# Beta's loads on ScalarE's queue, the feature maps as tasks of their own, and a smaller allowance when few scores are ready, in a four-layer attention kernel

## The chip, the cores and the metric

The kernel runs on one core of one Trainium2 chip. The metric is the device time of one execution in microseconds (us). The engines are named as in the profile: PE (TensorE, matmuls), DVE (VectorE), ACT (ScalarE), POOL (GpSimd) and SP (the queue that issues most DMAs). [...]

## The reference

The input x has 2048 tokens of 512 features. Four layers follow each other, A, B, A, B, each as x = x + f(layernorm(x)). Both kinds have 32 heads of 16 features.

```python
# layer A: four segments of 512 tokens, a memory M, z carried from one to the next
p = softmax(q @ k.T * 0.25 + causal_mask)          # inside the segment
a_dot = p @ v
phi = lambda t: where(t > 0, t + 1, exp(t))
a_mem = (phi(q) @ M) / (phi(q) @ z + 1e-6)
o = g * a_mem + (1 - g) * a_dot                    # g = sigmoid(beta), one number per head
M, z = M + phi(k).T @ v, z + phi(k).sum(tokens)
# layer B: plain attention over all 2048 tokens
o = softmax(q @ k.T * 0.25) @ v
```

Each layer ends with a product with its output weights. Gates g come from beta, 32 numbers.

## The kernel before, in words

The program is written out by a planner in Python: it appends instructions to five lists, one per engine, and derives the waits from the buffers that they read and write. What follows is the planner's order, which is also the order on each engine.

**Units.** The work is paced by units of three score banks. A bank is 128 keys by up to 512 queries of one head; PE computes it (line 325 in all cases, from masked queries `qm` and keys KA or KB), ACT takes the exponential of up to three banks at once (line 1023), and two or three units later PE multiplies with the values into bank 6. Score banks alternate between banks 0 to 2 and 3 to 5, so PE can be at most one unit ahead of ACT. Units of an A layer are causally masked: their banks are 512, 512 (two pieces) or 256 wide, and POOL cuts the diagonal (line 1038). Units of a B layer are unmasked and all 512 wide. Some banks of B layers ("dx") go to DVE instead, which computes the exponential with a polynomial (lines 732 and 756 to 766). When a group of a head's banks is done, DVE transposes the sum (line 1083), and POOL and DVE normalise it and write it to `oT` (lines 1087 to 1111).

**Background tasks.** All else is a task, a Python generator that yields `(needs, pe, dve)` ahead of each step: the needs that must be met, its PE bank use and its DVE cost in ns. `task_A` and `task_B` do LayerNorm, the transposes of the normalised x by DMA, and the projections of a segment. A projection is four matmuls into bank 7, the only bank for background work while units run, and a copy by DVE (line 341). `task_A` then also makes the feature maps phi(K) and phi(Q) (`phi`, line 510): ACT takes an exponential of half of them into `amem` (line 513), and two units later DVE combines it (lines 515 and 516). `task_mem` reads the memory and updates it (lines 577 to 631). `task_out` adds the memory's part and does the output projection into x (lines 664 to 693). A task list sorted by hand-written numbers (`make_tasks`, line 852) sets who is asked first; outputs come first of all, then earlier segments.

**Allowances.** After each unit `credit` (line 842) adds an allowance for PE and DVE; tasks run while it lasts. For unmasked units, tasks with a PE bank are asked first (`background(True)`, line 1202), the rest after. If fewer than 24 banks are ready the state is `low` (line 1195): no dx, and the allowance is 2600 ns of DVE a unit, instead of 1300 for A and 1420 for B units. Where a later instruction needs something that no task has done yet, `bg_must` (line 822) runs tasks on the spot; `run_deferred` (line 1101) uses it before it overwrites `oT`, if the output projection that reads it has not been written out.

**Start.** SP issues the first four tiles of x, the weights of A, then beta twice (once as `bet` for all partitions, in four pieces as `betT`, lines 368 to 374), then the rest of x and the other weights. `gates` (line 408) computes the two forms of the gates right after the first segment's transposes and ahead of the copies of its first projections: on ACT and on DVE these copies stand behind the gates. Before the first unit 66 matmuls on a unit matrix keep PE busy.

Of the kernel before, what the change touches and what calls it, by code (L numbers as in the profile page):

```python
# [7 lines left out]
P = 128  # L8
# [204 lines left out]
class Builder:  # L213
# [142 lines left out]

    def setup(self):
        sc = self.sc
        xv = self.inp["A_x"][0].rearrange("(t p) d -> p t d", p=P)
        for a, b in [(0, 1), (1, 2), (2, 3), (3, 4), (4, 8), (8, 12), (12, 16)]:  # L360
            sc.add_dma("sp", (lambda a, b: lambda e: e.dma_start(self.x[:, a:b, :], xv[:, a:b, :]))(a, b), self.batch(),
                       writes=self.b_x[a:b])
            if a == 3:
                for i, nm in ((1, "A_wk"), (0, "A_wq"), (2, "A_wv")):
                    src = self.inp[nm].rearrange("(c p) f -> p c f", p=P)
                    sc.add_dma("sp", (lambda i, src: lambda e: e.dma_start(self.wA[:, :, i * D:(i + 1) * D], src))(i, src),
                               self.batch(), writes=[self.b_wA[i]])
                beta = self.inp["A_beta"]
                sc.add_dma("sp", lambda e: e.dma_start(self.bet[:, :], beta.partition_broadcast(P)), self.batch(), writes=[self.b_bet])
                bb = self.batch()  # L370
                for r in range(4):
                    src = bass.AP(tensor=beta.tensor, offset=beta.offset + 2 * r, ap=[[0, 32], [8, 4], [1, 2]])
                    sc.add_dma("sp", (lambda r, src: lambda e: e.dma_start(self.betT[32 * r:32 * r + 32, :, :], src))(r, src),
                               bb, writes=[self.b_betT] if r == 3 else [])
        for w, b, nm in ((self.woA, self.b_woA, "A_wo"), (self.wB, self.b_wB[0], "B_wqkv"), (self.woB, self.b_woB, "B_wo")):
            src = self.inp[nm].rearrange("(c p) f -> p c f", p=P)
            sc.add_dma("sp", (lambda w, src: lambda e: e.dma_start(w[:, :, :], src))(w, src), self.batch(), writes=[b])

        def pool(fn, writes, reads=()):
            self.op("pool", fn, reads=reads, writes=writes)  # L380
        pool(lambda e: e.memset(self.ident[:, :], 1.0), [self.b_ident])
        pool(lambda e: e.affine_select(self.ident[:, :], self.ident[:, :], pattern=[[-1, P]], compare_op=ALU.is_equal,
                                       fill=0.0, base=0, channel_multiplier=1), [self.b_ident], [self.b_ident])
        wu = self.new_alloc()
        for _ in range(66):
            self.mm(self.ps[:, 0:P], self.ident[:, :], self.ident[:, :], True, True, [self.b_ident], self.banks[0], wu)
        hm = self.hmask
        pool(lambda e: e.memset(hm[:, :], 1.0), [self.b_hm])
        pool(lambda e: e.affine_select(hm[:, :], hm[:, :], pattern=[[-16, 8]], compare_op=ALU.is_ge,
                                       fill=0.0, base=0, channel_multiplier=1), [self.b_hm], [self.b_hm])  # L390
        pool(lambda e: e.affine_select(hm[:, :], hm[:, :], pattern=[[16, 8]], compare_op=ALU.is_ge,
                                       fill=0.0, base=15, channel_multiplier=-1), [self.b_hm], [self.b_hm])

        self.par = self.nc.alloc_sbuf_tensor("par", [P, 2], dt.float32)
        self.b_par = Buf("par")
        for e_ in range(2):
            hv = hm[:, :].rearrange("p (r two) -> p two r", two=2)[:, e_, :]
            self.op("dve", (lambda e_, hv: lambda e: e.tensor_reduce(self.par[:, e_:e_ + 1], hv, axis=mybir.AxisListType.X,
                                                                     op=ALU.add))(e_, hv),
                    reads=[self.b_hm], writes=[self.b_par])  # L400
        va = self.VA[:, :, :, :].rearrange("p s t (h f) -> p (s t) h f", f=17)
        pool(lambda e: e.memset(va[:, :, :, 16:17], 1.0), [b for l in self.b_VA for b in l])
        for bk in (6, 7):
            b = self.banks[bk]
            b.alloc = -1
            self.op("dve", (lambda b: lambda e: e.memset(self.ps[:, b.col0:b.col0 + 512], 0.0))(b), bank=b, alloc=-1)
# [103 lines left out]
    def phi(self, src, bsrc, dst, bdst):  # L510

        et = self.amem[:, :, :, :].rearrange("p a b c -> p a (b c)")
        self.op("act", lambda e: e.activation(et, src, ACT.Exp), reads=bsrc, writes=self.b_amem)  # L513
        yield [("at", self.step + 2)], 0, 1130
        self.op("dve", lambda e: e.tensor_scalar(dst, src, 0.0, 1.0, op0=ALU.max, op1=ALU.add), reads=bsrc, writes=bdst)
        self.op("dve", lambda e: e.tensor_tensor(dst, dst, et, ALU.min), reads=self.b_amem + bdst, writes=bdst)

    def v_evac(self, vt, bv):
        def f(bank, al, o):
# [5 lines left out]
    def task_A(self, L, s):  # L525
        sl = s % 2
# [8 lines left out]
        slot = self.take_xT()  # L535
# [6 lines left out]
        for c in range(NCH):  # L542
            yield from self.proj_fm(self.wA, self.b_wA[1], 512, slot, c, self.KA[:, sl, c, :], self.b_KA[sl][c])
            self.flags.add(("K", L, s, c))
            yield from self.proj_fm(self.wA, self.b_wA[0], 0, slot, c, self.QA[:, sl, c, :], self.b_QA[sl][c])
            self.flags.add(("Q", L, s, c))
            if c == 0:
                for ti in range(4):
                    yield from self.proj_tm(self.wA, self.b_wA[2], 1024, slot, ti,
                                            self.v_evac(self.VA[:, sl, ti, :], self.b_VA[sl][ti]))  # L550
                self.flags.add(("V", L, s))
        if s < 3:
            prev = (L, s - 1) if s else (L - 2, 3)
            read = [("dma", ("amemT",) + prev + (3,))] if prev[0] >= 0 and prev[1] else []
            yield ([("mem",) + prev] if prev[0] >= 0 else []), 0, 0
            old = [o for b in self.b_phk for o in b.reads.values()]
            for c in range(NCH):
                self.dma_tr(self.phk[:, :, c * 128:(c + 1) * 128], self.KA[:, sl, c, :], [self.b_KA[sl][c]], [self.b_phkc[c]],
                            ("phk", L, s), old)
            for j in range(2):  # L560
                yield [("dma", ("phk", L, s))] + read, 0, 0
                a, ba = self.phk[:, 2 * j:2 * j + 2, :], self.b_phk[2 * j:2 * j + 2]
                yield from self.phi(a, self.b_phkc + ba, a, ba)
            self.flags.add(("phk", L, s))
        self.give_xT(slot)
        if s > 0:
            for c in (0, 2):
                yield [("op", L, s - 1), ("mem", L, s - 1)] + ([("dma", ("amemT", L, s - 1, 3))] if s > 1 else []), 0, 0
                yield from self.phi(self.QA[:, sl, c:c + 2, :], self.b_QA[sl][c:c + 2], self.phq[:, c:c + 2, :], self.b_phq[c:c + 2])
            self.flags.add(("phq", L, s))  # L570
        self.flags.add(("proj", L, s))

    def task_mem(self, L, s):

# [207 lines left out]
    def met(self, need):  # L782
# [3 lines left out]
        def ok(n):  # L786
            if n == "xT":
                return len(self.xT_free) > 0
            if n == "xn":
                return done(("xn", self.rr.get("xn", 0) % 2))  # L790
            if n[0] == "dma":
# [60 lines left out]
    def make_tasks(self):  # L852
        order = []
        for base in (0, 2):
            A, B = base, base + 1
            for s in range(4):
                order.append((base * 100 + s * 10 + 1, self.task_A(A, s)))
                order.append((base * 100 + s * 10 + 2, self.task_mem(A, s)))
                order.append((base * 100 + s * 10 + (13 if base or s > 1 else 5), self.task_B(B, s)))
                order.append((-10, self.task_out(A, s)))  # L860
                order.append((-5, self.task_out(B, s)))
        order.sort(key=lambda z: z[0])
# [291 lines left out]
    def attention(self):  # L1154
        self.flags = {("x", 0, s) for s in range(NSEG)}
        self.xT_free = [0, 1]
        self.dma_at, self.forcing = {}, False
        self.sel, self.pvq, self.deferred, self.qm_free = [], [], [], [0, 1, 2, 3]
        self.qm_late = []

# [11 lines left out]
        n = 0  # L1172
        while True:
# [23 lines left out]
            isA = items[0][0].kind == "A"  # L1197
            split = not self.low and not isA
            self.unit(n, items, self.dx_pick(items))
            self.credit(5 if self.low else 2 if isA else 3, 2600 if self.low else 1300 if isA else 1420)  # L1200
            if split:
                self.background(True)
            self.cr_dve -= self.pv_step(n)
# [51 lines left out]
```

## Time and profile before

| | us |
|---|---|
| median of 3 runs (lowest, highest) | 2148.92 (2148.39, 2151.72) |
| the profiled execution, its own time | 2149.91 |
| its span, first to last instruction | 2148.0 |
| ACT busy in it | 2008.6 |
| PE busy | 1789.5 |
| DVE busy | 1593.3 |
| POOL busy | 407.0 |
| ACT waiting for PE's scores | 97.9 |
| mean granted PE clock | 0.694 |

A row of the profile's groups or timeline has the engine, the line of the kernel, the operation, what it writes and reads, and in brackets how long the engine sat idle before it and what ended that. The busy time of a merged row is the sum without overlaps. In the table by stages each stage has its length and then busy time and number of instructions for PE, PE's weight loads, DVE, ACT and POOL, then the granted PE clock, the share of the DMA engines' time, and GB/s. A wait row gives the sum, the number and the longest wait.

### The profile page before, as it was taken

To read this page: it belongs to the slowest core of one execution; us is meant where nothing else is said; L and a number is where in the kernel's file an instruction comes from. 1 tells how busy PE (TensorE), PEld (TensorE's weight loads), DVE (VectorE), ACT (ScalarE), POOL (GpSimd) and SP (SyncE) were. 2 spreads that over 40 slices of the span, in tenths; PEclk is the share of its full clock that TensorE was granted. 3 is DMA by queue.
4 is the path that set the end of the run, shared out by engine and by line. 5 is a ranking of instruction groups with operands and counts; after the bars stand their busy time and mean duration, and the time that the engine had idled before them with its cause. 6 is when DMAs were issued, how large, how long until landed. Compare 5 with 4: busy or idle time off the path is not lost.

```text
span 2148.0 us, 30875 instructions
## 1 busy us (share of the span) xinstructions
PE 1789.5 (83%) x11634; PEld 414.1 (19%) x11634; DVE 1593.3 (74%) x2806; ACT 2008.6 (94%) x1618; POOL 407.0 (19%) x832
## 2 busy tenths in 40 slices
PE   7788888888788787787877888888888888888888
PEld 3222222211211212212222112221111111111111
DVE  6655665487658885688857975548799989988996
ACT  5788998999989999899998998889999999999997
POOL 3532433020150002400033102501100000000000
PEclk9889888756957968769866558785655565556555
DMA  4011000000000000000000001000000000000000
GB/s 138 16 25 21 20 14 13 6 1 13 8 1 11 1 13 9 11 11 1 15 11 6 1 3 19 11 11 1 11 1 1 1 11 1 1 1 11 1 1 11
DMA packets 67125, 24.54 MB, mean 11 GB/s; under 512 B 59808, under 2 KB 66464, under 8 KB 66976
## 3 DMA queue, kind: packets, MB, share of 16 engines
q1 hardware_dynamic: 66976, 22.57, 4.6%
q8 instruction: 91, 1.49, 0.3%
q14 instruction: 58, 0.48, 0.1%
HBM read 6.30 MB, written 2.10 MB: 4 GB/s over the span
## 4 chain that ended last, share of the span: by engine, by line
issue 39%; ACT 28%; PE 19%; DVE 9%; POOL 4%; DMA 1%; SPq 0%; POOLq 0%; ACTq 0%; DVEq 0%
ACT pT L1023 27%; PE ps L325 19%; POOL ob L1096 1%; POOL pT L1038 1%; POOL qm L941 1%; DVE tT L1083 1%; DVE VB L341 1%; DVE VA L341 1%; DVE dxt L732 1%; DMA xT<-xn 1%; DVE QB L341 0%; ACT amem L513 0%; DVE x L686 0%; DVE lnst L431 0%; DVE QA L341 0%
## 5 line engine op out<-in xcount | busy, mean ns | idle before, releaser
L1023 ACT ACTIVATE pT<-ps 128x1536 bf16<-128x1536 f32 (+2 forms) x1589 | 1985.8, 1439 | 111.1 <-PE ps L325 97.9
L325 PE MATMUL ps<-qm,KB 32*128 32x512 bf16 x4096 | 682.5, 524 | 235.3 <-ACT pT L1023 217.6
L325 PE MATMUL ps<-pT,VB 128*17 128x512 bf16 x3716 | 664.8, 515 | 23.7 <-DVE tT L1083 18.3
L1096 POOL TENSOR_TENSOR ob<-tT,rd 128x256 bf16<-128x256 f32 x128 | 99.8, 780 | 1207.5 <-DVE rd L1087 1168.3
L732 DVE TENSOR_SCALAR dxt<-ps 128x512 uint32<-128x512 f32 x380 | 261.0, 687 | 86.3 <-PE ps L325 80.3
L325 PEld LDWEIGHTS ps<-qm,KB 32*128 32x128 bf16 x4096 | 133.8, 96 | 762.9 <-ACT pT L1023 679.6
L1038 POOL TENSOR_SCALAR_AFFINE_SELECT pT<-pT 128x256 bf16<-128x256 bf16 (+2 forms) x512 | 210.2, 427 | 322.4 <-ACT pT L1023 313.1
L766 DVE SCALAR_TENSOR_TENSOR dxo<-dxt,dxz 128x1024 int16<-128x1024 uint16 (+1 forms) x203 | 235.1, 1158 | 4.6
L325 PEld LDWEIGHTS ps<-pT,VB 128*17 128x17 bf16 x3716 | 119.1, 90 | 520.3 <-issue 452.9
L325 PE MATMUL ps<-dxo,VB 128*17 128x512 bf16 x380 | 205.4, 541 | 0.4 <-DVE dxo L766 0.4
L325 PE MATMUL ps<-qm,KA 32*128 32x512 bf16 (+3 forms) x1024 | 127.5, 376 | 39.6 <-ACT pT L1023 31.8
L760 DVE TENSOR_TENSOR dxz<-dxz,dxo 128x1024 f16<-128x1024 f16 (+1 forms) x203 | 135.1, 666 | 4.3
L325 PE MATMUL ps<-pT,VA 128*17 128x512 bf16 (+3 forms) x1024 | 121.2, 378 | 18.5 <-DVE tT L1083 10.9
L756 DVE TENSOR_SCALAR dxo<-dxt 128x1024 f16<-128x1024 uint16 (+1 forms) x203 | 132.9, 655 | 2.2 <-PE ps L325 2.0
L764 DVE TENSOR_TENSOR dxz<-dxz,dxo 128x1024 f16<-128x1024 f16 (+1 forms) x203 | 131.8, 649 | 2.1
L1083 DVE STREAM_TRANSPOSE tT<-ps 128x512 f32<-128x512 f32 x112 | 79.7, 712 | 70.6 <-PE ps L325 70.4
L941 POOL TENSOR_SCALAR qm<-QB,par 128x512 bf16<-128x512 bf16 x102 | 81.6, 808 | 180.2 <-PE ps L325 179.9
L758 DVE TENSOR_SCALAR dxz<-dxo 128x1024 f16<-128x1024 f16 (+1 forms) x203 | 88.7, 437 | 6.8
L325 PE MATMUL ps<-xT,wB 128*128 128x512 bf16 x256 | 82.9, 433 | 9.2 <-DMA xT<-xn 2.5
L686 DVE TENSOR_TENSOR x<-x,ps 128x512 bf16<-128x512 bf16 x64 | 44.0, 688 | 60.2 <-PE ps L325 60.0
L762 DVE TENSOR_SCALAR dxz<-dxz 128x1024 f16<-128x1024 f16 (+1 forms) x203 | 83.7, 412 | 6.7
L325 PE MATMUL ps<-xT,wA 128*128 128x512 bf16 x256 | 78.6, 419 | 10.3 <-DVE QA L341 5.3
(89 smaller groups left out, 917.9 us busy)
## 6 DMA issues: line engine op xcount, KB each, us to landing
out_dram<-x SPq DMA_DIRECT2D x8, 256.0 KB, 2.1
x<-in_A_x_dram SPq DMA_DIRECT2D x3, 512.0 KB, 10.9
wB<-in_B_wqkv_dram SPq DMA_DIRECT2D x1, 1536.0 KB, 12.7
xT<-xn SPq DMA_TRANSPOSE x60, 2.5
x<-in_A_x_dram SPq DMA_DIRECT2D x4, 128.0 KB, 2.4
wA<-in_A_wk_dram SPq DMA_DIRECT2D x1, 512.0 KB, 4.4
wA<-in_A_wq_dram SPq DMA_DIRECT2D x1, 512.0 KB, 5.5
wA<-in_A_wv_dram SPq DMA_DIRECT2D x1, 512.0 KB, 6.3
```

Of the source, the lines that this page charges most:

```text
L325: self.sc.add("pe", lambda e: e.matmul(out, lhsT, rhs, start=start, stop=stop, skip_group_check=True), reads=reads, banks=[(bank, "w", all ...
L732: self.op("dve", lambda e: e.tensor_scalar(self.dxt[:, b, i, :], o, SCALE * LOG2E * 65536, 127.0 * 65536, op0=ALU.mult, op1=ALU.add), writ ...
L756: self.op("dve", lambda e: e.tensor_scalar(f, lo, 2.0 ** -16, None, op0=ALU.mult), reads=bt, writes=bo)
L758: self.op("dve", lambda e: e.tensor_scalar(z, f, EXP_C3, EXP_C2, op0=ALU.mult, op1=ALU.add), reads=bo, writes=bz)
L760: self.op("dve", lambda e: e.tensor_tensor(z, z, f, ALU.mult), reads=bo + bz, writes=bz)
L764: self.op("dve", lambda e: e.tensor_tensor(z, z, f, ALU.mult), reads=bo + bz, writes=bz)
L766: self.op("dve", lambda e: e.scalar_tensor_tensor(ob, hi, 128.0, z, op0=ALU.mult, op1=ALU.add), reads=bt + bz, writes=bo)
L941: self.op(eng, (lambda m, q, col: lambda e: e.tensor_scalar(m, q, col, 0.0, op0=ALU.mult, op1=ALU.add))(m, q, col), reads=[bq, self.b_par] ...
L1023: self.sc.add("act", (lambda dst, src: lambda e: e.activation(dst, src, ACT.Exp, scale=SCALE))(dst, src), writes=self.b_pT[slot * 3 + i:sl ...
L1038: self.op("pool", (lambda blk, pat: lambda e: e.affine_select(blk, blk, pattern=pat, compare_op=ALU.is_ge, fill=0.0, base=0, channel_multi ...
L1083: self.op("dve", lambda e: e.transpose(tT.rearrange("p a b -> p (a b)"), src), reads=bsrc, writes=[bt], bank=bk, alloc=al)
L1096: self.op("pool", lambda e: e.tensor_tensor(ob, tT[:, :, 0:16], rb, ALU.mult), reads=[bt, br], writes=[self.b_ob[oi][g.e]])
```

## The change

1. The five loads of beta are issued by ACT as its first instructions, instead of by SP between the weights and the rest of x.
2. The feature maps leave `task_A` for a task of their own, `task_phi`, sorted right behind it. A half may begin only two units after the half before it was combined (`"phi"`). `task_A` gives its buffer of transposed x back before the feature maps rather than after those of K. Layer 1's tasks for segments 0 and 1 are now asked ahead of `task_phi` and `task_mem` of the same segment; before they were asked behind `task_mem`.
3. In the state `low` the allowance is 1900 ns of DVE a unit instead of 2600.

```diff
     def setup(self):
         sc = self.sc
+        beta = self.inp["A_beta"]
+        bb = self.batch()
+        for r in range(4):
+            src = bass.AP(tensor=beta.tensor, offset=beta.offset + 2 * r, ap=[[0, 32], [8, 4], [1, 2]])
+            sc.add_dma("act", (lambda r, src: lambda e: e.dma_start(self.betT[32 * r:32 * r + 32, :, :], src))(r, src),
+                       bb, writes=[self.b_betT] if r == 3 else [])
+        sc.add_dma("act", lambda e: e.dma_start(self.bet[:, :], beta.partition_broadcast(P)), self.batch(), writes=[self.b_bet])
...
-                sc.add_dma("sp", lambda e: e.dma_start(self.bet[:, :], beta.partition_broadcast(P)), self.batch(), writes=[self.b_bet])
-                bb = self.batch()
-                for r in range(4):
-                    src = bass.AP(tensor=beta.tensor, offset=beta.offset + 2 * r, ap=[[0, 32], [8, 4], [1, 2]])
-                    sc.add_dma("sp", (lambda r, src: lambda e: e.dma_start(self.betT[32 * r:32 * r + 32, :, :], src))(r, src),
-                               bb, writes=[self.b_betT] if r == 3 else [])
...
         self.op("dve", lambda e: e.tensor_tensor(dst, dst, et, ALU.min), reads=self.b_amem + bdst, writes=bdst)
+        self.phi_at = self.step
...
+        self.give_xT(slot)
+        self.flags.add(("KQ", L, s))
+
+    def task_phi(self, L, s):
+
+        sl = s % 2
+        yield [("KQ", L, s)], 0, 0
         if s < 3:
...
-                yield [("dma", ("phk", L, s))] + read, 0, 0
+                yield [("dma", ("phk", L, s)), "phi"] + read, 0, 0
...
-        self.give_xT(slot)
         if s > 0:
             for c in (0, 2):
-                yield [("op", L, s - 1), ("mem", L, s - 1)] + ([("dma", ("amemT", L, s - 1, 3))] if s > 1 else []), 0, 0
+                yield ["phi", ("op", L, s - 1), ("mem", L, s - 1)] + ([("dma", ("amemT", L, s - 1, 3))] if s > 1 else []), 0, 0
...
+            if n == "phi":
+                return self.bubble or self.forcing or self.step >= self.phi_at + 2
...
-                order.append((base * 100 + s * 10 + 2, self.task_mem(A, s)))
-                order.append((base * 100 + s * 10 + (13 if base or s > 1 else 5), self.task_B(B, s)))
+                order.append((base * 100 + s * 10 + 2, self.task_phi(A, s)))
+                order.append((base * 100 + s * 10 + 3, self.task_mem(A, s)))
+                order.append((base * 100 + s * 10 + (14 if base or s > 1 else 1.5), self.task_B(B, s)))
...
-            self.credit(5 if self.low else 2 if isA else 3, 2600 if self.low else 1300 if isA else 1420)
+            self.credit(5 if self.low else 2 if isA else 3, 1900 if self.low else 1300 if isA else 1420)
```

The arithmetic is the same. The changed program has the same operations but for the planner's choices: 376 instead of 380 banks go to DVE.

More of the change, by code (lines that the diff above doesn't have):

```diff
@@ L367, in setup @@
                                self.batch(), writes=[self.b_wA[i]])
-                beta = self.inp["A_beta"]
-                sc.add_dma("sp", lambda e: e.dma_start(self.bet[:, :], beta.partition_broadcast(P)), self.batch(), writes=[self.b_bet])
-                bb = self.batch()
-                for r in range(4):
-                    src = bass.AP(tensor=beta.tensor, offset=beta.offset + 2 * r, ap=[[0, 32], [8, 4], [1, 2]])
-                    sc.add_dma("sp", (lambda r, src: lambda e: e.dma_start(self.betT[32 * r:32 * r + 32, :, :], src))(r, src),
-                               bb, writes=[self.b_betT] if r == 3 else [])
         for w, b, nm in ((self.woA, self.b_woA, "A_wo"), (self.wB, self.b_wB[0], "B_wqkv"), (self.woB, self.b_woB, "B_wo")):
@@ L564, in task_A @@
             self.flags.add(("phk", L, s))
-        self.give_xT(slot)
         if s > 0:
             for c in (0, 2):
-                yield [("op", L, s - 1), ("mem", L, s - 1)] + ([("dma", ("amemT", L, s - 1, 3))] if s > 1 else []), 0, 0
+                yield ["phi", ("op", L, s - 1), ("mem", L, s - 1)] + ([("dma", ("amemT", L, s - 1, 3))] if s > 1 else []), 0, 0
                 yield from self.phi(self.QA[:, sl, c:c + 2, :], self.b_QA[sl][c:c + 2], self.phq[:, c:c + 2, :], self.b_phq[c:c + 2])
             self.flags.add(("phq", L, s))
-        self.flags.add(("proj", L, s))
     def task_mem(self, L, s):
@@ L1156, in attention @@
         self.xT_free = [0, 1]
-        self.dma_at, self.forcing = {}, False
+        self.dma_at, self.forcing, self.phi_at = {}, False, -9
         self.sel, self.pvq, self.deferred, self.qm_free = [], [], [], [0, 1, 2, 3]
```

## The prediction, made before the changed kernel ran

> **What bounds the kernel now.** I read the page first, then ScalarE's (ACT's) waits, then the busy time of each stage, then the timeline of the stages that lose time. The page says which engine sets the end:
>
> ```profile
> span 2148.0 us, 30875 instructions
> ...
> PE 1789.5 (83%) x11634; PEld 414.1 (19%) x11634; DVE 1593.3 (74%) x2806; ACT 2008.6 (94%) x1618; POOL 407.0 (19%) x832
> ```
>
> ACT works 2008.6 of 2148.0 us, nearly all of it exponentials of scores. So the time is ACT's work plus ACT's idle time, 139.4 us, and an edit counts only as far as it changes one of the two. ACT's waits name what ends the idle time:
>
> ```profile
> ACT pT L1023 <- PE ps L325: 97.9, 137, 4.2
> ...
> ACT omgT L414 <- DMA betT<-in_A_beta_dram: 5.0, 1, 5.0
> ...
> ACT amem L513 <- DVE phk L516: 3.3, 2, 3.0
> ```
>
> Mostly scores come late from TensorE (PE); the wait for beta and the wait of one half feature map for the other are the two that the change aims at. The table by stages shows where the idle time lies (a stage's length less its ACT column; PEclk is the granted clock):
>
> ```profile
> 17.80:32.06 14.26, 11.87 (x66) 3.24 (x65) 9.00 (x24) 7.92 (x7) 3.98 (x11) 0.78 0.64 217
> ...
> 90.72:129.03 38.31, 26.62 (x177) 6.66 (x177) 25.64 (x64) 23.16 (x26) 19.24 (x49) 0.79 0.14 28
> 129.03:344.60 215.57, 186.38 (x1334) 50.76 (x1334) 125.85 (x262) 192.79 (x181) 77.04 (x184) 0.82 0.11 21
> ...
> 578.73:624.01 45.28, 34.52 (x268) 9.31 (x270) 20.33 (x43) 39.74 (x43) 32.34 (x79) 0.52 0.00 1
> ...
> 1145.74:1406.78 261.04, 221.96 (x1415) 50.18 (x1410) 184.52 (x328) 242.89 (x199) 53.91 (x107) 0.70 0.04 7
> ```
>
> Idle: 14.7 us before the first score at 17.80, then 6.3, 8.8 (to 90.72), 15.2, 22.8, and 18.2 in the last row. The long stage 1441 to 2137 idles 3.7 of 695 us, so nothing can be won there. I follow the change by units (unit n is the n-th set of three score banks); the order of the changed program's instructions tells what PE and VectorE (DVE) do between two units.
>
> **Start, units 0 to 5.**
>
> ```profile
> 10.93 1.89 PE L325 MATMUL ps<-xT,wA 128*128 128x512 bf16 x8 [0.87 <-DVE gtok L416]
> ...
> 15.62 0.21 ACT L414 ACTIVATE omgT<-betT 128x8 f32<-128x8 bf16 x1 [5.02 <-DMA betT<-in_A_beta_dram]
> 15.73 0.58 ACT L339 ACTIVATE QA<-ps 128x512 bf16<-128x512 f32 x1
> ...
> 17.14 0.61 PE L325 MATMUL ps<-qm,KA 32*128 32x512 bf16 x3 [4.32 <-DVE qm L941]
> 17.69 1.89 PE L325 MATMUL ps<-wA,xT 128*128 128x512 bf16 x4
> 17.80 1.45 ACT L1023 ACTIVATE pT<-ps 128x1536 bf16<-128x1536 f32 x1 [1.49 <-PE ps L325]
> ```
>
> Behind the exponential that waits for betT stand QA's copy on ACT and, on DVE, KA's copy and the masked queries. The Q projection ends at 10.93+1.89 = 12.8. With beta there, QA's copy ends at 13.4, the first masked query 0.4 later, scores follow at 13.9 instead of 17.14, and the first exponential at 14.4: 3.4 us earlier. What is late next is PE itself. Its pause shrinks from 4.3 to 1.1 us. In this trace the clock is 0.50 from 17.1 to 23.9 and 1.00 after; at 0.50 the four V matmuls take 1.89 and the scores 0.61, later 1.04 and 0.39. Three units at the full clock save 3 x (0.85+0.22) = 3.2. Together -6.6; walking the new DVE order (three operations a unit for the next segment's statistics, not five to nine) through these durations puts unit 6 at 25.4 instead of 32.06, the same. The other end: ACT now issues five DMAs first, 0.5 us each by SP's rows, over long before its first work at 9.45; SP loses five issues, so x's later tiles start some 2.9 us earlier, which nothing waits for. But bet lands at 4.25+5.9 = 10.2 and the last betT at 15.6: four transfers of 0.5 KB take 5.4 us. If they hold up the first four x tiles (issued from 0.8 to 2.2, 2.4 us to landing) by half of it, 2.7, the term is -3.9; by all of it, 5.4, the first score comes at 19.8 at the low clock: +2.
>
> [...]
>
> **Feature maps, halves apart.** Row 3.3+0.4 us of ACT waits. 3.0 of it is unit 59: there the scores for unit 60 ended at about 121.0 while ACT was free at 119.7, so 1.3 stays: -1.8. (Bounds 0 and -3.7.)
>
> **Smaller allowance.** Around 92 to 102 us PE waits 4.25 for QA's copy behind the next layer's LayerNorm on DVE; ACT loses 4.2+2.8+1.5 = 8.5. The new order has 28 DVE operations in five units where 29 stood in four. By their durations QA's copy ends at 95.9, the next scores at 97.7, and 6.7 is still lost: -1.7 (bounds +2, -6).
>
> **What the own task moves.** A half map needs 1130 of the DVE allowance; in unmasked units tasks with a PE bank are served first and spend it. So in segments 1 and 2 of layer 0 the last half map waits until the next masked units: the memory steps move from units 75 and 147 to 97 and 161, and the output projection, which came one a unit, must now be forced before oT is overwritten: in the new order sixteen woA matmuls stand in a row, twice; nowhere before. What one costs:
>
> ```profile
> 164.34 1.04 PE L325 MATMUL ps<-woA,oT 128*128 128x512 bf16 x4
> ...
> 165.41 0.69 DVE L686 TENSOR_TENSOR x<-x,ps 128x512 bf16<-128x512 bf16 x1 [0.27 <-PE ps L325]
> ...
> 166.16 1.04 PE L325 MATMUL ps<-woA,oT 128*128 128x512 bf16 x4
> ```
>
> One bank, so four matmuls, DVE's addition, the next four: a period of 1.82. Four end after 3 x 1.82+1.04 = 6.5; with weighted sums and the next scores (0.95) less one exponential (1.35), ACT idles 6.1. Two projections within one unit near 1312 cost ACT 2.51,
>
> ```profile
> 1311.65 1.04 PE L325 MATMUL ps<-wA,xT 128*128 128x512 bf16 x4 [0.54 <-DVE VA L341]
> ...
> 1313.48 1.04 PE L325 MATMUL ps<-wA,xT 128*128 128x512 bf16 x4 [0.79 <-DVE VA L341]
> ...
> 1315.14 2.43 ACT L1023 ACTIVATE pT<-ps 128x512 bf16<-128x512 f32 x3 [2.51 <-PE ps L325]
> ```
>
> and the same sum gives 1.82+1.04+0.8-0.96 = 2.7 for them. Two bursts 12.2, less the 2.1 that the spread outputs cost now: +10.1. Memory steps 1 and 2 stand among masked units, whose exponentials are shorter (1.2 a unit): step 3, which stands so now, costs 2.8, those among unmasked units 0.2. I take 1.8 each, +3.2; step 3 moves the other way, -2. Layer 0's projections of segments 2 and 3 move to unmasked units: by the idle before the units concerned 6.6 to 3.6, -3; layer 1's, with more whole projections in one unit, +0.7 and -1. Stage sum +8 (bounds +2, +17).
>
> **Layer 2.** Its memory steps 1 and 2 begin 7 units later and lie partly among unmasked units: idle 2.0+6.2 to about 5.7, -2.5 (0, -4). In the stage from 1146 the doubled projections of 1312 no longer occur (-2.5), one start after a pause goes (-1.3), and memory step and projections interleave at half a projection a unit (4.8 to 3.1): -5.5 (0, -8).
>
> **ACT's own work.** Counting the order: 376 scores on DVE instead of 380, so 4 more banks on ACT, and other cuts of the masked units: +9 of 1024 columns, +10 of 256, +10 of 768, +2 of 1536, -40 of 512. With 1.04, 0.40, 0.83, 1.36 and 0.54 us a piece: +2.8; by columns alone +1.8. I take +2.
>
> **Sum.** -6.6-1.8-1.7+8-2.5-5.5+2 = -8.1. The profiled execution took 2149.9 (span 2148.0 and 1.9 around it), 1.0 above the median of 2148.92; so 2141.8 by its own time and 2140.8 by the median. I forecast 2141. About 0.2%, 4.3 us, can be told from no change.
>
> **Rivals.**
> 1. Held-up start: the first term is -0.4 to +2 instead of -6.6, 2147 to 2150. For it: 5.4 us for 2 KB. Against: only what comes before the fourth tile's landing near 4.6 matters, when not all four can be through.
> 2. Layer 2 gives nothing (the dx queries on POOL, 2.3 to 3.6 a stage there, remain): -0.1, 2149.
> 3. The low clock, on the slow side: the moved stretch loses PE's clock. After each burst some ten units carry no projection, and such stages show 0.52 (578 to 624) though PE is 76% busy. At the low clock a burst costs 4 x 2.67-0.8 = 9.9 before scores, 9.5 idle: +6.8; memory steps 3 each, +2.4; the seven whole projections a unit from unit 130 at 2.67 instead of 1.82, +5.9. -8.1+15.1 = +7.0, 2156. It decides once bursts and projections both run cold (+12.7; +12.4 is the point for slower).
> 4. The change does not do what it says: the order shows all three parts done; only the halves' distance grows to 17 units.
>
> [...]
>
> **Chances.** Forecast, 2133 to 2146: 0.58; held-up start 0.13; layer 2 0.14; low clock 0.12; else 0.03. Faster 0.60, within 0.2% 0.27, slower 0.13. The range 2133 to 2151 takes in the first three.
>
> **What would show it.** Right: first exponential near 14.4 and clock 1.00 from 14 to 24; two ACT waits of about 6 where sixteen woA matmuls stand; no wait of amem for phk; idle in the stage that ends with unit 205 near 31, from 1146 on near 13. Wrong: x's first four tiles landing after 6 us, bursts with 1.89 a projection, or ACT work off by over 3.

## The result and the profile after

The changed kernel takes 2171.7 us (median of six runs, 2166.9 to 2178.9) beside 2151.6 for the kernel before: a ratio of 1.0097, 95% interval 1.0077 to 1.0118. It is 1% slower. I had forecast 2141 and a range that ended at 2151.

The profiled execution took 2166.89, the least of the six; its span is 2165.2, 17.2 us more than before, while the medians lie 20.1 apart. The first rows of the profile's page say whether ScalarE (ACT) worked longer or waited longer:

```profile
span 2165.2 us, 30735 instructions
...
PE 1782.1 (82%) x11539; PEld 418.4 (19%) x11634; DVE 1581.5 (73%) x2790; ACT 2011.8 (93%) x1609; POOL 400.8 (19%) x828
```

ACT works 3.2 us more than before and idles 153.4 us instead of 139.4. So the loss is idle time, as the bound of the prediction wants it. The table by stages, cut at the same units as in the prediction (the columns are those of that table), shows where:

```profile
18.75:30.16 11.41, 9.01 (x65) 2.88 (x64) 9.00 (x24) 7.80 (x8) 4.47 (x11) 1.00 0.55 202
88.63:122.96 34.33, 25.00 (x176) 6.58 (x177) 23.31 (x54) 22.33 (x25) 18.65 (x48) 0.85 0.16 32
122.96:360.57 237.61, 191.98 (x1308) 52.77 (x1326) 125.37 (x269) 193.19 (x171) 77.31 (x183) 0.76 0.10 19
...
597.04:642.06 45.02, 34.84 (x268) 9.42 (x270) 20.68 (x43) 39.79 (x43) 32.44 (x79) 0.54 0.00 1
1164.09:1419.00 254.91, 214.96 (x1418) 51.88 (x1428) 177.83 (x321) 243.32 (x192) 51.40 (x109) 0.75 0.04 8
```

A row's length less its ACT column is ACT's idle time: 3.6 (6.3 before), 12.0 (15.2), **44.4 (22.8)**, 5.2 (5.5) and 11.6 (18.2). Every one of these rows but one got better. The long stage of units 64 to 205 got worse by 21.6, and that is the result. In elapsed time against the kernel before, cut at the same units:

| part of the program | forecast | measured |
|---|---|---|
| until the first exponential of scores | -3.4 | +1.0 |
| units 0 to 63 | -6.7 (-3.2, -1.8, -1.7) | -7.0 |
| units 64 to 295 | +8 | **+23.6** (+22.0 to unit 205, +1.5 after) |
| units 296 to 1047 (the rest of layer 1, layer 2) | -2.5 and -5.5 | -5.4 (+1.8 to unit 746, -7.2 after) |
| the last 450 units, and ACT's own work | +2 | +5.1 |
| sum | -8.1 | +17.2 |

**The start.** On ACT's queue beta does come first, and x pays for it: its first four tiles land 4.7 us (median) after their issue, 2.4 in the kernel before. Rows of the first 19 us of the changed kernel (its line 1032 is line 1023 of before, 950 is 941, 692 is 686), and behind them the row of the kernel before in which the statistics of the fourth tile of x start:

```profile
0.80 1.87 ACTq L363 DMA_DIRECT2D betT<-in_A_beta_dram  x4
...
7.23 0.69 DVE L431 BATCH_NORM_STATS2 lnst<-x 128x6 f32<-128x512 bf16 x1 [1.02 <-DMA x<-in_A_x_dram]
...
11.15 1.03 PE L329 MATMUL ps<-ident,xn 128*128 128x128 bf16 x8 [3.42 <-DVE xn L464]
...
11.98 1.06 PE L329 MATMUL ps<-ident,oT 128*128 128x128 bf16 x8
...
14.30 2.94 PE L325 MATMUL ps<-xT,wA 128*128 128x512 bf16 x7 [1.26 <-DVE omgT L416]
...
17.28 0.60 ACT L339 ACTIVATE QA<-ps 128x512 bf16<-128x512 f32 x1 [3.81 <-PE ps L325]
...
18.75 1.45 ACT L1032 ACTIVATE pT<-ps 128x1536 bf16<-128x1536 f32 x1 [0.88 <-PE ps L325]
```

```profile
5.73 0.66 DVE L431 BATCH_NORM_STATS2 lnst<-x 128x6 f32<-128x512 bf16 x1
```

VectorE (DVE) waits for the third tile of x until 7.23, where it had all four by 5.73 before. TensorE (PE) pauses for 3.4 us instead of 0.8 after its 66 matmuls, and its clock falls (0.50 from 10.0 to 16.8 us): the transposes take 1.03 and 1.06 instead of 0.72 and 0.72, and the seven projection matmuls that the trace has take 2.94, 0.42 each, where eight took 1.89.

**The two rows of sixteen woA matmuls (the bursts) and one more wait.** First the stretch of unit 109, then SP's queue ahead of unit 127, then the stretch of unit 173:

```profile
190.85 1.04 PE L325 MATMUL ps<-woA,oT 128*128 128x512 bf16 x4 [0.78 <-DVE x L692]
191.92 0.69 DVE L692 TENSOR_TENSOR x<-x,ps 128x512 bf16<-128x512 bf16 x1 [1.13 <-PE ps L325]
...
194.15 10.77 ACT L1032 ACTIVATE pT<-ps 128x1536 bf16<-128x1536 f32 x11 [5.97 <-PE ps L325]
...
214.98 2.50 SPq L348 DMA_TRANSPOSE xT<-xn  x2
217.58 5.14 SPq L348 DMA_TRANSPOSE phk<-KA  x4
...
224.15 1.06 ACT L513 ACTIVATE amem<-phk 128x1024 bf16<-128x1024 bf16 x1 [4.37 <-issue]
...
299.28 1.89 PE L325 MATMUL ps<-woA,oT 128*128 128x512 bf16 x4 [0.78 <-DVE x L692]
...
301.95 1.89 PE L325 MATMUL ps<-woA,oT 128*128 128x512 bf16 x4 [0.78 <-DVE x L692]
...
307.17 9.62 ACT L1032 ACTIVATE pT<-ps 128x1536 bf16<-128x1536 f32 x10 [9.47 <-PE ps L325]
```

Four matmuls, DVE's addition, the next four: a period of 1.82 in the first burst, 2.67 in the second, where the clock is at 0.50. ACT waits 5.97 and 9.47. Between them stands a wait that I had not seen coming: ACT's exponential of phi(K) waits 4.37, though the profile names no engine for it ("issue"). The rows above it tell what it is: the four transposes into phk occupy SP's queue from 217.58 to 222.7, and they stand there behind two transposes of another task, from 214.98 to 217.48. KA, which they read, had long been there: the order has its last projection in unit 101 and the request in unit 124.

### The profile page after: what moved, and what is told of

Read it like the earlier page. It is cut to its first block, busy times and chain, and to the rows that moved or that the text cites. A ratio compares the mean times of both kernels' runs of the same rounds, so it can differ in the third digit from the quotient of the medians.

```text
span 2165.2 us, 30735 instructions
## 1 busy us (share of the span) xinstructions
PE 1782.1 (82%) x11539; PEld 418.4 (19%) x11634; DVE 1581.5 (73%) x2790; ACT 2011.8 (93%) x1609; POOL 400.8 (19%) x828
## 4 chain that ended last, share of the span: by engine, by line
issue 40%; ACT 27%; PE 18%; DVE 10%; POOL 4%; DMA 1%; SPq 0%; ACTq 0%; POOLq 0%; DVEq 0%
ACT pT L1032 27%; PE ps L325 18%; POOL pT L1047 2%; POOL ob L1105 1%; POOL qm L950 1%; DVE tT L1092 1%; DVE dxt L738 1%; DVE VB L341 1%; DVE QB L341 1%; DVE VA L341 1%; DVE x L692 1%; DVE KA L341 1%; DVE KB L341 1%; ACT amem L513 1%; DVE QA L341 0%
## 5 line engine op out<-in xcount | busy, mean ns | idle before, releaser
L1032 ACT ACTIVATE pT<-ps 128x1536 bf16<-128x1536 f32 (+3 forms) x1580 | 1990.5, 1441 | 123.2 <-PE ps L325 113.1
L325 PE MATMUL ps<-qm,KB 32*128 32x512 bf16 x4096 | 690.1, 521 | 239.4 <-ACT pT L1032 221.7
L1047 POOL TENSOR_SCALAR_AFFINE_SELECT pT<-pT 128x128 bf16<-128x128 bf16 (+2 forms) x512 | 210.4, 426 | 368.4 <-ACT pT L1032 359.0
L325 PE MATMUL ps<-dxo,VB 128*17 128x512 bf16 x376 | 199.7, 531 | 0.0
L325 PE MATMUL ps<-qm,KA 32*128 32x384 bf16 (+3 forms) x1024 | 128.3, 378 | 33.4 <-ACT pT L1032 31.5
L325 PE MATMUL ps<-pT,VA 128*17 128x384 bf16 (+3 forms) x1024 | 123.2, 381 | 18.1 <-DVE tT L1092 14.4
L325 PE MATMUL ps<-xT,wB 128*128 128x512 bf16 x232 | 73.6, 418 | 16.1 <-DMA xT<-xn 2.9
L325 PE MATMUL ps<-xT,wA 128*128 128x512 bf16 x230 | 73.0, 425 | 12.2 <-DVE QA L341 3.0
## 6 DMA issues: line engine op xcount, KB each, us to landing
wA<-in_A_wv_dram SPq DMA_DIRECT2D x1, 512.0 KB, 11.5
```

The costliest lines, as they stand in the source:

```text
L325: self.sc.add("pe", lambda e: e.matmul(out, lhsT, rhs, start=start, stop=stop, skip_group_check=True), reads=reads, banks=[(bank, "w", all ...
L1032: self.sc.add("act", (lambda dst, src: lambda e: e.activation(dst, src, ACT.Exp, scale=SCALE))(dst, src), writes=self.b_pT[slot * 3 + i:sl ...
L1047: self.op("pool", (lambda blk, pat: lambda e: e.affine_select(blk, blk, pattern=pat, compare_op=ALU.is_ge, fill=0.0, base=0, channel_multi ...
```

## The experiments

Every group of runs (E1 to E4, E5 to E8, E9 to E12) was made on one chip, with runs of the kernel before on that chip; its median was 2150.5, 2148.4 and 2154.3 in the three groups, so kernels are compared by their ratios to it, with 95% intervals. Each kernel has one trace.

**E1, the first part alone** (the beta transfers on ACT's queue; the diff is the first half of the change's).

> The kernel before with the first part alone: the five transfers of beta requested on ScalarE's queue ahead of everything, nothing else. The order of every engine's work is that of before. Theory (held-up start, small): in the changed kernel's profile the first exponential came at 18.75 us instead of 17.80, but units 0 to 5 then took 11.4 us instead of 14.3, because the clock stayed at 1.00; so this part alone should put unit 6 near 30.2 instead of 32.1 and give about 2150 beside 2151.6 (ratio 0.999). Rival (the start is a large part of the loss, and of the scatter of 12 us between the changed kernel's runs): 2155 to 2162, runs far apart. What I forecast at first (-6.6) would give 2145.

Measured: 2153.8, ratio 1.0014 (1.0002 to 1.0026). The first exponential of scores comes at 19.1, and unit 64 at 130.2, 1.2 us later than in the kernel before. So the first part is a small loss by itself, and faster units 0 to 5 do not come with it for certain: they take 14.2 us here, in the order of before, where the clock stays at 0.50 from 11.3 to 28.4, and 11.4 in the changed kernel, where it does so only from 10.0 to 16.8. The runs lie 10 us apart, and those of the kernel before beside them 11 (2145.5 to 2156.1): the scatter is no mark of the change.

**E2, the third part alone.**

```diff
-            self.credit(5 if self.low else 2 if isA else 3, 2600 if self.low else 1300 if isA else 1420)
+            self.credit(5 if self.low else 2 if isA else 3, 1900 if self.low else 1300 if isA else 1420)
```

> The kernel before with the third part alone: VectorE's allowance per unit where few scores are ready 1900 instead of 2600. Theory: memory steps and output projections stay where they are in the kernel before (units 75 to 82 and 147 to 154, one output projection a unit), so there is no burst of woA matmuls; units 46 to 63 lose about 3 us less idle time; there is one more unit at the end (1496) with a few more columns on ScalarE, +2. About 2150 (ratio 0.999). Rival (the allowance is what moved the work and made the loss): 2165 or more.

Measured: 2157.2, ratio 1.0031 (1.0021 to 1.0041): neither theory. Units 0 to 63 gain 3.1 us in the profile, as forecast, but units 205 to 295 lose 4.0 (the state of few ready scores lasts from unit 205 to 212 instead of one unit), and the last layer loses 4.8, half of it more work of ACT and half idle time. The program has one unit more, as I had said; what it costs is more than the 2 that I gave it.

**E3, the second and third parts** (the changed kernel with beta back on SP's queue).

> The changed kernel with the beta transfers put back on SP's queue behind the weights (the second and third parts alone). Theory (own task with halves two units apart makes the loss): as slow as the changed kernel or 2 us slower, 2172 to 2174, with two stretches of sixteen woA matmuls that cost ScalarE 6 to 9.5 us each. Rival (the start makes the loss or the scatter): 2160 or less, runs within 6 us.

Measured: 2170.6, ratio 1.0094 (1.0074 to 1.0115), the same as the changed kernel's. Beta's place is not the loss. The profile gives something better than the time. The order of the second burst is the same, but the clock rose from 0.50 to 1.00 while it ran, at 298.4:

```profile
301.76 1.04 PE L325 MATMUL ps<-woA,oT 128*128 128x512 bf16 x4 [0.78 <-DVE x L692]
...
305.06 1.45 ACT L1032 ACTIVATE pT<-ps 128x1536 bf16<-128x1536 f32 x1 [6.13 <-PE ps L325]
```

6.13 at the full clock, 9.47 at half of it: the low clock is worth 3.3 us in a burst. The order does not settle which of them one gets: E6 below has both bursts in this order once more, and there ACT waits 6.8 and 9.5.

**E4, without the spacing of the halves** (own tasks, the allowance and beta's queue as changed).

```diff
-                yield [("dma", ("phk", L, s)), "phi"] + read, 0, 0
+                yield [("dma", ("phk", L, s))] + read, 0, 0
...
-                yield ["phi", ("op", L, s - 1), ("mem", L, s - 1)] + ([("dma", ("amemT", L, s - 1, 3))] if s > 1 else []), 0, 0
+                yield [("op", L, s - 1), ("mem", L, s - 1)] + ([("dma", ("amemT", L, s - 1, 3))] if s > 1 else []), 0, 0
```

> The changed kernel without the condition that two half maps lie two units apart; own tasks, beta's queue and the allowance stay as changed. In its order the memory steps of segments 1 and 2 of layer 0 return to units 75 to 82 and 147 to 154, and no burst of sixteen woA matmuls is left. Theory (the spacing makes the loss): ScalarE's idle time between units 64 and 208 falls from 45 to about 24 us; the gain of 7 us around unit 900 goes too, so about 2153 (2150 to 2156). Rival (the own task or the loss is elsewhere, say in the clock of the whole stage): 2165 or more.

Measured: 2154.1, ratio 1.0024 (1.0009 to 1.0039), as the theory has it; the twelve runs spread over 14 us (2150.7 to 2164.8). The 0.24% that is left is less than E1 and E2 cost by themselves (0.14% and 0.31%), so the own task itself shows no cost; the condition that halves lie two units apart makes the loss.

**E5, the spacing taken out only where it moves the memory steps.**

```diff
+        apart = ["phi"] if L or s not in (1, 2) else []
...
-                yield [("dma", ("phk", L, s)), "phi"] + read, 0, 0
+                yield [("dma", ("phk", L, s))] + apart + read, 0, 0
```

(the same `apart` in the place of the second "phi").

> The changed kernel, but in segments 1 and 2 of layer 0 the halves need not lie two units apart; everywhere else they do. The memory steps of these segments return to units 75 to 82 and 147 to 154, the two stretches of sixteen woA matmuls are gone, and layer 2 keeps its changed order. Theory (the displaced memory steps and the forced output projections are the loss, and layer 2 keeps a gain of 7): ScalarE's idle time between units 64 and 208 falls from 45 to 24..29 us, about 2153 (2149 to 2157). Rival (layer 2 gains nothing in the mean of several runs): 2156 to 2161.

Measured: 2143.0, ratio 0.9976 (0.9967 to 0.9985): less than the 2149 that was the least expected, faster than the kernel before, and 1.2% faster than the changed kernel, for one condition in two of eight segments. ACT's idle time by ranges of units, in the three traces:

| units | before | E5 | changed |
|---|---|---|---|
| 108, 109 and 172, 173 (the bursts) | 0.4 | 0.4 | 17.4 |
| 120 to 146 | 1.4 | 1.1 | 11.5 |
| 64 to 202 without these | 20.7 | 18.2 | 13.0 |

The bursts cost 17.0, the 27 units between them 10.2, and elsewhere the changed kernel gains 7.7.

**E6, the spacing taken out in layer 2 only** (`apart = ["phi"] if not L else []`).

> The changed kernel, but in layer 2 the halves need not lie two units apart; in layer 0 they do, so both bursts stay. Layer 2's projections, memory steps and outputs stand again where they stand in the kernel before. Theory: the stage from 1146 us on loses its gain of 7 us, so 2171 + 5 to 7 = 2176 to 2178. Rival (layer 2's order is worth nothing): 2169 to 2173.

Measured: 2176.3, ratio 1.0132 (1.0119 to 1.0145), 0.35% or 7.5 us above the changed kernel's ratio. Layer 2's share of the forecast is real: in the changed kernel the stretch of units 747 to 1047 is 7.2 us shorter than before, here it is 0.8 shorter. Other traces have the same two orders of instructions in this stretch: with the spacing it took 425.1, 426.7 and 426.8 us (the changed kernel, E3, E5), without it 428.1 to 435.2 (before, E1, E7, E8, E9).

**E7 and E8, beta elsewhere** (both the kernel before with another place for beta). In E7 ACT requests it, but only when x's fourth tile has landed; in E8 SP does, between x's tiles and the weights.

```diff
             if a == 3:
+                for r in range(4):
...
+                    sc.add_dma("act", (lambda r, src: lambda e: e.dma_start(self.betT[32 * r:32 * r + 32, :, :], src))(r, src),
+                               bb, reads=[self.b_x[3]], writes=[self.b_betT] if r == 3 else [])
```

(E8: "sp" instead of "act" and no reads; in both the lines of beta behind the weights go.)

> The kernel before with beta requested on ScalarE's queue as in the change, but only once x's fourth tile has landed; the order of the engines' work is that of before. Theory (beta's 720 small packets held up x's first tiles, and nothing else was wrong with the first part): the four tiles land as in the kernel before (the last statistics end near 6.6 us, not 9.0), there is no pause of 3.4 us in PE's work ahead of the transposes, betT is there by 11 to 13 us, the first exponential starts at 14.5 to 15.5 instead of 17.8, and unit 6 starts 3 to 6 us earlier: 2145 to 2148 beside 2150.5. Rival (the small packets are slow whenever they run beside the weights, 7 us or more to landing): the first exponential stays at 17 to 18, time that of before.

> The kernel before with beta's five transfers on SP's queue directly behind x's first four tiles, ahead of the weights, at 2.6 us instead of 4.25. Theory: x's tiles, already under way, lose less than 1 us; the weights are requested 2.4 us later, wk at 5.1, and land 2 us later, before they are needed at 10.9; betT lands by 8 to 11 us; first exponential at 14.4 to 15.5, 2145 to 2148. Rival (the packets of beta hold up tiles that are under way as well): last statistics later than 8 us, first exponential 17 to 19, 2150 to 2154.

Measured: E7 2156.4, ratio 1.0040 (1.0024 to 1.0055); E8 2149.1, ratio 1.0000 (0.9992 to 1.0009). Neither theory holds, and the rivals hold in part. E7 is worse than its rival: the tiles come in time, but bet lands at 18.0, 11 us after its request, beside the weights and the rest of x, and the first exponential of scores is at 20.6. In E8 that exponential is at 17.9, where the rival has it, but not for the rival's reason: the tiles come in time and beta is there at 11.2, but the weights are late, and PE waits for them:

```profile
13.19 3.19 PE L325 MATMUL ps<-xT,wA 128*128 128x512 bf16 x7 [3.12 <-DMA wA<-in_A_wk_dram]
...
17.46 0.39 PE L325 MATMUL ps<-qm,KA 32*128 32x512 bf16 x3 [1.08 <-DVE qm L941]
```

wk takes 7.7 us to land, 4.4 in the kernel before. In all four places of beta's five transfers something is late: ahead of x it is x (4.7 us to landing instead of 2.4), ahead of the weights it is the weights (wk's 7.7 instead of 4.4), and beside or behind the weights it is beta itself (bet at 18.0 in E7, betT at 15.6 in the kernel before).

**E9, the transfers of betT taken away** (from the kernel before). bet holds every beta on every partition already, so the second form of the gates is computed from it. bet's one transfer is requested between x's four tiles and the weights, where E8 had all five; the cut shows the gates.

```diff
+            pieces = [(d2, s2)]
+            if neg:
+                bv = self.bet[:, :].rearrange("p (c r j) -> p c r j", r=4, j=2)
+                pieces = [(self.omgT[32 * r:32 * r + 32, :, :], bv[32 * r:32 * r + 32, :, r, :]) for r in range(4)]
...
```

> The kernel before, but the four transfers of betT are gone: omgT is computed from bet, which holds every beta on all partitions, by four exponentials of 32 partitions x 8 (0.2 us each) instead of one of 128 x 8, and bet is requested on SP's queue directly behind x's four tiles, one transfer, 0.5 us ahead of the weights. Theory (the start is bound by what the DMA engines carry: beta's small packets hold up x when they go first and the weights when they go second, so only fewer packets help): wk and wq land as in the kernel before (before 9), no exponential waits for beta, the first exponential at 14.0 to 15.0 instead of 17.8, unit 6 at 26 to 29 instead of 32; 2144 to 2147 beside 2148.4 to 2151. Rival (the start is bound elsewhere, as in the run with beta behind x, which gave nothing): first exponential at 17 or later, time that of before.

Measured: 2142.2, ratio 0.9945 (0.9932 to 0.9959), more than expected. Rows of ACT's start:

```profile
10.49 0.91 ACT L414 ACTIVATE omgT<-bet 32x8 f32<-32x8 bf16 x4
12.86 0.60 ACT L339 ACTIVATE QA<-ps 128x512 bf16<-128x512 f32 x1 [1.46 <-PE ps L325]
14.34 2.79 ACT L1023 ACTIVATE pT<-ps 128x1536 bf16<-128x1536 f32 x2 [0.88 <-PE ps L325]
```

The first exponential of scores comes at 14.34; the prediction's 14.4 was the time without a hold-up. Unit 6 starts at 27.0 instead of 32.1, unit 64 at 123.4 instead of 129.0. These 5.7 us are about half of the 12 between the medians; where the rest lies is not shown, since there is no trace of the kernel before from this group.

**E10, the version with all amendments, and E12, the same with beta first on ACT's queue.** Both are the changed kernel with E5's condition and with the small allowance only in the first 65 units; E10 has E9's gates and E9's place for bet too. The cut shows the allowance.

```diff
-            self.credit(5 if self.low else 2 if isA else 3, 1900 if self.low else 1300 if isA else 1420)
+            self.credit(5 if self.low else 2 if isA else 3, 1900 if self.low and self.step < 66 else 2600 if self.low else 1300 if isA else 1420)
```

> The changed kernel with three amendments: no spacing in segments 1 and 2 of layer 0 (no bursts), the allowance of 1900 only in the first 65 units (2600 in later units with few scores ready), and the gates from one tile as above. Theory: 2143.0 of the run without spacing in segments 1 and 2, less 2 to 4 for the low units 205 and 960 on, less 3 to 4 for the start: 2135 to 2139. Rival (the three do not add): 2141 to 2144.

> As the best version, but with beta's five transfers first on ScalarE's queue, as in the change: no spacing in segments 1 and 2 of layer 0, allowance of 1900 only in the first 65 units. Theory (the smaller allowance costs 2 to 4 us at the low units 205 to 212 and 960 to 975, where it only ends in more scores on ScalarE): 2139 to 2141. Rival (the allowance there does nothing in this order): 2143.

Measured: E10 2139.7, ratio 0.9931 (0.9918 to 0.9943), the fastest; E12 2142.3, ratio 0.9942 (0.9930 to 0.9955). E10 lies between its theory and its rival, E12 near its rival. The gains do not add: over E12 the new gates bring 2.6 us, though over the kernel before they brought 12. E10 is only a little faster than E9: their intervals overlap, but four of its five runs lie below all five of E9, and the medians are 2.5 us apart. What the restricted allowance brings over E5 is not settled. E5 ran on another chip; the two traces differ by 2.5 us, but E12 is 3.2 ahead already at unit 6 (29.4 beside 32.6), which the restriction does not reach, and the last layer, in the order of the changed kernel, takes 621.8 us in E12, 622.1 in the changed kernel and 620.0 in E5.

**E11, a burst without the rest of the change.** The kernel before, in which the output projection of segment 1 of layer 0 is held back until it is forced.

```diff
+            if L == 0 and s == 1:
+                need.append("forced")
             yield need, 4, 700
```

> The kernel before, with the output projection of segment 1 of layer 0 held back until it must be run ahead of the write to oT: four projections stand in one row at unit 108 and four more, with four additions, at unit 151, while the half maps and the first memory step stay where they are (unit 75 to 82). Nothing else of the change is in it. Theory (a burst costs 6.1 at the full clock and 9.5 at the low one, whoever makes it): ScalarE waits 6 to 10 us at units 109 and 152 each, and the kernel is 10 to 20 us slower, 2160 to 2170. Rival (the displaced memory steps, not the outputs, make the loss): waits below 4 us, 2150 to 2155.

Measured: 2199.1, ratio 1.0207 (1.0193 to 1.0221), more than either theory. The first burst stands alone, its memory step still at units 75 to 82:

```profile
207.94 2.36 ACT L1027 ACTIVATE pT<-ps 128x1536 bf16<-128x1536 f32 x2 [9.48 <-PE ps L325]
```

9.48, with 1.89 for four matmuls: the price of the changed kernel's second burst to 0.01 us, at the same low clock and without a displaced memory step. The later bursts cannot be read for it: ACT waits 18.0 at unit 142 and 31.2 at 152, where other tasks that the held projection had blocked are forced as well.

## Why the prediction was wrong

**The bound was right.** Idle time of ACT decided, and the stages that I worked through are those in which it changed.

**The step that failed is the sum "What the own task moves", +8.** It measured +22.0 in the units that it was made for, 64 to 205, outside the bounds that I gave it (+2, +17). Its mechanism was right: the order showed the memory steps displaced and the output projections forced, and E5 took that away and is 1.2%, 26 us, faster. The sizes were off in three terms:
- The two bursts: 12.2 forecast, 17.0 measured. The first is right (6.1 forecast, 5.97). The second ran at the low clock: 9.47, which the third rival had at 9.5, and 1.5 stands in the unit ahead of it. I gave the low clock 0.12 as one case for both bursts; here it met one of two, as in E6, and in E3 neither in full.
- The units 120 to 146: I had layer 0's and layer 1's projections there at -3, +0.7 and -1, and measured +10.2. 4.4 of it is the wait for phk's transposes. The planner gives a transfer three units; in unmasked units of 1.4 us that is 4.2. On SP's queue the two transposes ahead took 2.5 and these four 5.1, and then they had to land, 1.4 more. In the kernel before 27 units lay between the request and its use in that segment, in the changed order three. I had counted how far the steps move and not how close a request had come to its use. The other 6 are waits for scores of up to 1.4 us each in units of which the first half ran mostly at 0.50. E5 shows that they come with the spacing; none of them was taken away by itself, so their division stays an account read from the trace.
- The memory steps: +3.2 forecast, no cost seen. The units that they left (75 to 82, 147 to 154) and those that they went to (97 to 107, 161 to 171) idle 4.1 us in all, 6.2 in the kernel before; projections left some of these units too, so this is no clean price.

**The first term failed as well: -6.6 forecast to unit 6; there the changed kernel's trace is 1.9 us earlier than before, E1's 1.2 later.** The first rival came true in kind, a held-up start. The size of the hold-up was right (2.7 taken for the half of it; the last tile's statistics end 2.5 later), and E9 shows that the chain behind it was (14.34 for 14.4). What I left out is what a late tile does to PE: its pause grew to 3.4 us, the clock was at 0.50 from 10.0 on, and transposes and projections took another 2.0 (0.5 and 1.5). That makes 14.4 + 2.5 + 2.0 = 18.9, and 18.75 was measured.

In these traces transfers of one queue held up those of another: x's first tiles took 4.7 us to land beside the transfers on ACT's queue (the changed kernel), 2.4 without them (the kernel before).

**What was right, and what was luck.** Units 0 to 63 gained 7.0 for 6.7, in the trace by the terms forecast: 2.9 in units 0 to 5 for 3.2, and 4.2 in units 6 to 63 for 3.5. The first of these is in part luck. With beta first on ACT's queue and the same order of work, units 0 to 5 took 11.4 us in three traces (the changed kernel, E6, E12), where the clock was back at 1.00 by 16.8, and 13.5 and 13.6 in two (E4, E5), where it came back at 25.1 and 25.4. E3, without the first part, gains 7.2 in units 0 to 63 all the same, 6.0 of it in units 6 to 63, and E1, with it alone, 0.1. Layer 2 gained 7.2 in its last stage for 5.5, and E6 loses about as much without the spacing; the 2.5 in its earlier stages did not come. ACT's own work was forecast at +2 and measured at +3.2. With the last layer's waits it makes +5.1, and E2 shows that the allowance alone makes 4.8 there.

## What to carry to other kernels

When a step of a background task may come later, look for what will be forced because of it: the gain is spread over hundreds of units, and the forced work stands in one place, in front of the engine that sets the end. Price such a burst at both clocks, and count for each moved request how long it now has until its use and what stands ahead of it in its queue. Here, where several loads competed at the start, another queue or place only chose which of them was late; four transfers fewer helped (E9, ratio 0.9945).

## What the hardware showed

**Ten KB of beta held up a megabyte in the first 8 us.** The profile's page counts 720 packets and 0.01 MB for the queue of these five transfers. The first 8 us of the changed kernel, of the kernel before, and of E8, where they stand between x's tiles and the weights:

```profile
0.00:8.00 8.00, 6.31 (x66) 6.14 (x66) 3.77 (x10) 1.28 (x1) 2.26 (x10) 1.00 0.31 78
```

```profile
0.00:8.00 8.00, 6.45 (x66) 6.28 (x66) 5.43 (x19) 1.28 (x1) 2.27 (x10) 1.00 0.70 222
```

```profile
0.00:8.00 8.00, 6.05 (x66) 5.88 (x66) 5.44 (x19) 1.28 (x1) 2.26 (x10) 1.00 0.25 66
```

78 GB/s with them in front and 222 with them behind is 1.15 MB less. The DMA engines were not full meanwhile: 0.31 of their time is taken with them in front, 0.70 with them behind. In E8, between x's tiles and the weights (4.5 to 9.0 us), they move 1 GB/s and are busy for 0.05 of the time. What such packets wait for is not shown.

**The clock stayed low under a busy PE.** The 12 us ahead of the second burst in the changed kernel, and the burst:

```profile
284.00:296.30 12.30, 11.06 (x86) 4.10 (x85) 7.23 (x16) 8.40 (x10) 7.59 (x18) 0.50 0.12 24
296.30:307.20 10.90, 8.22 (x28) 1.96 (x26) 3.44 (x7) 1.43 (x2) 2.85 (x10) 0.50 0.00 1
```

PE is busy by the profile's count for 11.06 of 12.30 us, 90%, and the granted clock is 0.50 all the while. The trace's record of the clock has it at 0.50 from 279.7 to 320.6; in E3, with the same order, it rose at 298.4. Why it did not rise in these 12 us is not shown. At the start of the changed kernel it fell in a pause: PE's 3.4 us without work begin at 7.7, and the clock is at 0.50 from 10.0, 2.3 us into them.
